# A new order table, four first transfers and 16 first fillers in a fused attention and gated-MLP kernel

## The chip, the core and the metric

The kernel runs on one core of one Trainium2 chip. The metric is the device time of one execution in microseconds; lower is better. The engines are named as in the profile: PE is TensorE (PEld its weight loads), DVE is VectorE, ACT is ScalarE, POOL is GpSimd, SP is SyncE, which only issues DMAs. DMAs that ScalarE issues show as ACTq, those of SP as SPq.

## What is computed

Attention with four sink positions and a window of 128, on 4 batches of 8 heads, 768 positions and 64 dimensions, then a gated MLP on its output (cut from the reference):

```python
scores = scale * np.matmul(q, k.transpose(0, 1, 3, 2))
keep = (pos[None, :] < n_sink) | ((rel >= 0) & (rel < window))      # n_sink 4, window 128
a = softmax(np.where(keep, scores, -1e9))
x = np.matmul(a, v)                       # -> (4, 768, 512)
h = np.maximum(x @ w_in, 0.0)             # 512 -> 1024
u, v = h[..., :512], h[..., 512:]
v_n = (v - mean(v)) / np.sqrt(var(v) + 1e-06)
v_s = np.einsum('ts,bsd->btd', w_spatial, v_n) + b_spatial[None, :, None]
out = (u * v_s) @ w_out                   # 512 -> 512
```

## The kernel before

**Stages.** A batch has six blocks of 128 positions; a step is one block and four of the eight heads, 48 steps in all. For each step TensorE makes the score products (L776) from `kring`, a ring of four blocks of keys and queries; VectorE adds the mask and takes the minimum (`mask`, L781); ScalarE takes the exponential (`exp`, L786); the result is split into a high and a low half of 16 bits (`p high`, `p low`, the low one at L511), turned by DMA transposes that SP issues (L852), and multiplied with `v` (`av`, L900). VectorE divides (L908), and the block `x` is split and turned in the same way. Steps 0 to 3 are turned on TensorE (`p cross`, `x cross`) instead. Then follow, for each block, `ps_v` = x @ w_in (its second half), `v relu`, `v stats` (L1005), `v root` on POOL (L1012), `v norm` (L1015: subtract the mean, multiply with the root), and the halves `vn high` and `vn low`; and, by chunks of 256 positions and 128 columns, `ps_u` (L529), `u relu` (L1049), `ps_s` with the spatial weights (L529), `gate` (L1072, adds the bias, on VectorE), `times` (L1076), `g high` (L679 on VectorE and POOL, L677 on ScalarE), `g low` (L1084), the output product `ps_o` (L1099), its copy `o copy` into a buffer `ob` (L1112, on ScalarE) and its store. The weights come in as `dec`, and are split into halves as well. Beside that stand tests of the inputs (`w check`, `v check`) whose result, the check, picks a general path at the end when the fast one would not be exact (it is not taken here).

**Rooms.** `ps_v`, `ps_u`, `ps_s`, `ps_o` and the turns on TensorE share two PSUM banks. `vr`, `ob` and two kinds of scratch (`junk`, `wtmp`) share a ring of three buffers in SBUF. A tile takes the room of an earlier one, and its first writer waits for the last reader of that one.

**What sets the order.** All work between the first loads and the end is recorded as 1799 pieces, numbered as they are recorded, each with the engines that can do it. The string `ORDER` lists them: a word is the number of a piece and the letter of its engine (P is TensorE, d VectorE, a ScalarE, p POOL, S SP). `Plan.order` walks it, and each engine's queue holds its pieces in this order; an engine whose next piece waits does nothing else. The costs given to `plan.add` aren't used when the kernel is built. A number behind P asks for as many fillers ahead of the piece: `warm` (L440) issues dummy matmuls of 128 x 248 into the bank of the piece itself, or of the piece named behind the colon. The first keys and queries are loaded ahead of everything else (L1190), by one DMA on SP's queue (head pairs 0 and 1) and one on ScalarE's (pairs 2 and 3).

Of the kernel before, what the change touches and what calls it, by code (L numbers as in the profile page):

```python
# [13 lines left out]
ALU = mybir.AluOpType  # L14
# [4 lines left out]
DM, DFF = 512, 1024  # L19
P = 128  # L20
# [179 lines left out]
NS = 4  # L200
# [4 lines left out]
NEG = -1.0e30  # L205
# [16 lines left out]
def cost(e, n, two=False, pointer=False):  # L222

    if e == "a":
        return 0.1 + n / 1200 + (0.1 if pointer else 0)
    if e == "d":
        return 0.085 + n / (960 if two else 1920) + (0.05 if pointer else 0)
    return 0.17 + n * 0.0018 if two else 0.14 + n * 0.001
# [5 lines left out]
116S 120P20 121d 123d 125d 117S 118p 257p 156p 119p 107S 108a 109a 21S 126a 127d 128a 111S 112a 110d 132P6:131  # L234
137d 139d 122a 124a 129P3 135d 22a 23d 133d 113a 136a 24d 25p 209p 114d 155S 159P1:131 164d 162d 140a 166d 130a
138a 134a 42S 141P2 160d 43a 44d 165a 115S 45d 46p 14S 131P 16d 163a 173P 180d 178d 174d 167a 161a 168P 142a 26a
176d 170P 143P 17d 15a 18p 208S 212P 144d 213d 215d 181a 217d 219d 179a 28S 30d 169a 47a 48d 313p 171a 154S 157p
0S 2d 177a 175a 216a 29a 31d 32p 214a 3d 184P15 218a 220a 185a 223a 1a 4p 182P 228P 233d 221a 183d 224d 235d 231d
229d 7S 9d 8a 35S 37d 236a 36a 207S 210a 230a 10d 11p 234a 256S 232a 239a 240p 225d 172P 145P 186P 187d 237a 49S
260P5 261d 38d 146a 50a 51d 39p 311S 314a 267d 33a 12a 188P9 189a 58S 263d 222S 265d 266a 241d 158d 211d 190a  # L240
268a 226S 255S 147P 148a 262a 264a 271a 269a 191d 52d 53p 272p 34d 276P 279d 258a 280a 227P 283d 284a 281d 282a
277d 192P 259d 273d 315d 312S 316P 319d 323d 321d 242S 317d 238S 243P 244d 245P23 278a 285a 289p 332P 287a 288p
5a 360S 6d 54a 40a 41d 27d 55d 270S 274S 275P 324a 322a 318a 339d 320a 193a 325a 286S 290S 246a 503S 327a 19a
333d 337d 340a 338a 334a 199P 326S 335d 247d 361p 364P 329p 328d 330S 336a 343a 344p 341a 13d 20d 504p 505p 345p
367d 368a 365d 200a 371d 369d 291P 56S 359S 292d 149d 342S 150p 151p 201P 346S 202a 380P 381d 550p 366a 370a 372a
373a 377p 57S 387d 383d 385d 382a 384a 194d 195p 293P 386a 294a 295d 375a 196p 248P 376d 508P 515d 513d 331P 509d
# [999 lines left out]
```

## Time and profile before

| | |
|---|---|
| three runs | 401.38, 401.75, 401.91 us (median 401.75) |
| the profiled execution | 401.43 us, span 399.6 us |
| busy in the span | PE 97%, DVE 78%, ACT 63%, POOL 53% |
| TensorE's mean granted clock | 0.999 of 2.4 GHz |
| fillers | 84, of which 20 ahead of the first score |

The span runs from the first to the last instruction. Each engine works through its own queue in order, so its idle time is read together with what ended it: in a timeline row the brackets give the idle time before the instruction and the engine, tile and line that released it. In the view of waits the releaser is the one that came last by the profile. Busy time of TensorE includes the fillers.

### The profile page before, as it was taken

The page shows a single profiled execution, that of the slowest core. Times are in us where ns is not written, and L with a number is a line of the kernel's source. Part 1 is how long each engine was busy: PE and PEld are TensorE (multiplying, and loading weights), DVE is VectorE, ACT ScalarE, POOL GpSimd, SP SyncE. Part 2 cuts the span into 40 slices and gives each one's busy share as a digit, 9 for nine tenths or more (in the row PEclk, how much of TensorE's full clock was granted, in tenths as well). Part 3 has the DMA queues.
Part 4 walks back from the last instruction along what each step waited for, and adds up shares of the span by engine and source line. Part 5 has one row for each costly group of instructions (what it writes and reads, how often), then busy time and mean ns, then how long its engine had stood idle before and what let it go on. Part 6 is the DMA issues. An engine that isn't in the chain of part 4 may idle for free. (4 is left out here: it accounts for less than half of the span.)

```text
span 399.6 us, 9923 instructions
## 1 busy us (share of the span) xinstructions
PE 387.3 (97%) x3697; PEld 276.4 (69%) x3697; DVE 312.4 (78%) x924; ACT 250.8 (63%) x553; POOL 210.5 (53%) x237
## 2 busy tenths in 40 slices
PE   7999998998999999999999999999999998999995
PEld 4785866686786774677777666777768666486773
DVE  3899999879888787989798897989896998342421
ACT  3999897877879476688796979888621131101010
POOL 4463596874552526454515478499666392720000
PEclk9999999999999999999999999999999999999999
DMA  6999999999895998869888979899799653001021
GB/s 194 384 284 218 196 183 230 256 251 219 205 228 135 242 188 192 214 153 144 165 173 210 207 186 267 143 189 147 168 237 232 185 175 85 27 2 53 2 80 57
DMA packets 137733, 70.96 MB, mean 178 GB/s; under 512 B 112080, under 2 KB 125392, under 8 KB 137680
## 3 DMA queue, kind: packets, MB, share of 16 engines
q1 hardware_dynamic: 136864, 70.02, 77.9%
q8 instruction: 30, 0.49, 0.5%
q10 hardware_dynamic: 816, 0.26, 0.3%
q14 instruction: 23, 0.19, 0.2%
HBM read 36.71 MB, written 6.29 MB: 108 GB/s over the span
## 5 line engine op out<-in xcount | busy, mean ns | idle before, releaser
L529 PE MATMUL ps_s<-wsp,vn 128*128 128x256 f16 x864 | 100.3, 273 | 0.7 <-ACT ob L1112 0.7
L786 ACT ACTIVATE pexp<-pexp,nm 128x260 f32<-128x260 f32 (+1 forms) x192 | 85.3, 484 | 18.6 <-DVE nm L781 18.2
L529 PEld LDWEIGHTS <-vn 128*128 128x128 f16 x864 | 83.1, 98 | 14.1 <-issue 2.2
L511 POOL TENSOR_TENSOR p<-pexp,p 128x1024 f16<-128x1024 f32 (+2 forms) x43 | 54.8, 1280 | 44.7 <-ACT p L495 35.7
L529 PE MATMUL ps_u<-xT,win 128*128 128x256 f16 x576 | 68.8, 273 | 1.6 <-DVE g L1072 1.1
L1099 PE MATMUL ps_o<-wout,g 128*128 128x512 f16 x276 | 62.9, 379 | 0.7 <-ACT ob L1112 0.7
L529 PEld LDWEIGHTS <-win 128*128 128x128 f16 x576 | 55.0, 98 | 11.4 <-issue 3.9
L529 PE MATMUL ps_v<-win,xT 128*128 128x512 f16 x264 | 60.5, 380 | 0.1
L1099 PEld LDWEIGHTS <-g 128*128 128x128 f16 x276 | 26.3, 98 | 30.1 <-issue 1.6
L776 PE MATMUL sc<-kring 64*128 64x260 f16 (+3 forms) x480 | 44.7, 312 | 1.3 <-DMA kring<-qk_t 1.2
L529 PEld LDWEIGHTS <-xT 128*128 128x128 f16 x264 | 24.8, 98 | 28.5 <-issue 1.5
L495 ACT CAST p<-pexp 128x32 f16<-128x32 f32 (+2 forms) x69 | 42.7, 639 | 2.7 <-DMA pT<-p 2.0
L1072 DVE SCALAR_TENSOR_TENSOR g<-ps_s,b_bc 128x256 f32<-128x256 f32 x48 | 20.2, 420 | 28.7 <-PE ps_s L529 28.6
L1015 POOL TENSOR_SCALAR vr<-vr,mv,rs 128x512 f32<-128x512 f32 x18 | 38.4, 2136 | 0.8
L1076 POOL TENSOR_TENSOR g<-g,u 128x256 f32<-128x256 f32 x22 | 17.4, 792 | 33.8 <-DVE g L1072 33.1
L1049 ACT ACTIVATE u<-ps_u 128x256 f32<-128x256 f32 x34 | 12.8, 378 | 34.2 <-PE ps_u L529 34.1
L900 PE MATMUL av<-vring,pT 128*128 128x65 f16 x328 | 34.2, 194 | 0.0
L901 PE MATMUL av<-vring,pT 128*128 128x65 f16 x328 | 34.1, 193 | 0.0
L902 PE MATMUL av<-vring,pT 128*128 128x65 f16 x328 | 34.1, 193 | 0.0
L511 DVE TENSOR_TENSOR p<-pexp,p 128x1024 f16<-128x1024 f32 (+2 forms) x33 | 27.0, 820 | 6.3 <-ACT p L495 6.2
L900 PEld LDWEIGHTS <-pT 128*128 128x128 f16 x328 | 30.3, 97 | 1.8 <-issue 0.8
L1084 DVE SCALAR_TENSOR_TENSOR g<-g,g 128x256 f16<-128x256 f16 x48 | 23.0, 484 | 10.0 <-POOL g L679 7.1
(144 smaller groups left out, 693.4 us busy)
## 6 DMA issues: line engine op xcount, KB each, us to landing
vraw<-v_s SPq DMA_DIRECT2D x30, 260.0 KB, 4.1
raw<-qk_t SPq DMA_DIRECT2D x12, 512.0 KB, 4.1
out<-ob SPq DMA_DIRECT2D x23, 256.0 KB, 2.3
kring<-qk_t SPq DMA_DIRECT2D x11, 512.0 KB, 5.6
dec<-w_in SPq DMA_DIRECT2D x8, 512.0 KB, 8.1
pexp<-w_in SPq DMA_DIRECT2D x8, 512.0 KB, 4.4
wsp<-w_sp_t SPq DMA_DIRECT2D x6, 384.0 KB, 4.1
dec<-w_out SPq DMA_DIRECT2D x4, 512.0 KB, 4.6
```

What stands on the lines that cost most here:

```text
L495: nc.scalar.copy(o, x)
L511: eng[e].tensor_tensor(out=o, in0=x, in1=hi, op=ALU.subtract)
L529: nc.tensor.matmul(o, a, m, start=(i == 0), stop=(i == n - 1))
L776: nc.tensor.matmul(view(h + q)[0], qq[:, hp, 1, 2:], keys, start=(j == 0), stop=(j == len(pairs) - 1))
L786: nc.scalar.activation(po, po, AF.Exp, bias=nm()[:, q:q + 1], scale=-1.0)
L900: nc.tensor.matmul(o[:, h], ph, vh, start=(t < 2 and j == 0), stop=False)
L901: nc.tensor.matmul(o[:, h], ph, vl, start=False, stop=False)
L902: nc.tensor.matmul(o[:, h], pl, vh, start=False, stop=(j == nb - 1 and (t < 2 or h == HH - 1)))
L1015: eng[e].tensor_scalar(vr(), vr(), vals["mv", i][:, 0:1], vals["rs", i], op0=ALU.subtract, op1=ALU.mult)
L1072: nc.vector.scalar_tensor_tensor(out=g(), in0=tl("ps_s", i)[:, :TC], scalar=G_S, in1=b_bc[:, t0:t0 + TC], op0=ALU.mult, op1=ALU.add)
L1084: plan.add("g low", r, b, "d", cost("d", TC, True), lambda e: nc.vector.scalar_tensor_tensor(out=g2()[:, 1], in0=g2()[:, 0], scalar=-2.0 * ...
L1099: nc.tensor.matmul(o, lead, wout[:, w, d, :], start=(d == 0 and j == 0), stop=(d == KC - 1 and j == 2))
```

## The change

`ORDER` is a new table: other places, and for some pieces another engine. In all DVE has 615 pieces (596 before), ACT 489 (508), POOL 213, PE and SP as many as before. By kind: `v norm` DVE 11 and POOL 13 (6 and 18 before); `p low` DVE 25 and POOL 19 (20 and 24); `vn high` ACT 6, DVE 6, POOL 12 (13, 3, 8); `vn low` DVE 6, POOL 18 (10, 14); `g high` ACT 16, DVE 16 (23, 9), POOL 16 as before; `u relu` ACT 32, DVE 16 (34, 14); `times` DVE 28, POOL 20 (26, 22). There are 65 fillers at eleven places (84 at nine): 16, 8, 1, 1, 6, 2, 5, 8, 1, 13 and 4, after 20, 6, 3, 1, 2, 15, 5, 9 and 23. On TensorE the order changes by neighbours changing places; from the output products of batch 2's second chunk on, about 328 us in the trace of before, it is the same. The costs in the code are set to other numbers. The first keys and queries come by four DMAs of 128 KB, one for each pair of heads, on SP's and ScalarE's queues in turn. The mask of the first block is made by one instruction on 124 columns. The line numbers after are one lower from L374 on. Of the table and of the costs one line each stands here:

```diff
-116S 120P20 121d 123d 125d 117S 118p 257p 156p 119p 107S 108a 109a 21S 126a 127d 128a 111S 112a 110d 132P6:131
+116S 120P16 127d 128a 117S 118p 125d 123d 21S 22a 23d 107S 121d 124a 132P8:143 139d 137d 111S 126a 108a 122a
...
-    def cur_mask(m):
-        nc.gpsimd.affine_select(out=m, in_=m, pattern=[[-1, P]], compare_op=ALU.is_ge,
-                                fill=NEG, base=0, channel_multiplier=1)
+    def cur_mask(m, first=0):
+        nc.gpsimd.affine_select(out=m, in_=m, pattern=[[-1, P - first]], compare_op=ALU.is_ge,
+                                fill=NEG, base=-first, channel_multiplier=1)
...
-    cur_mask(m_first)
-    nc.gpsimd.memset(m_first[:, :NS], 0.0)
+    cur_mask(m_first[:, NS:], NS)
...
-            plan.add("v norm", r, b, "dp", {"d": 0.46, "p": 0.75}, norm, [("st", i)], [("vr", i)], shared=True)
+            plan.add("v norm", r, b, "dp", {"d": 0.47, "p": 2.05}, norm, [("st", i)], [("vr", i)], shared=True)
...
-            for e, hs in ((nc.sync, slice(0, HP // 2)), (nc.scalar, slice(HP // 2, HP))):
-                e.dma_start(kring[:, 0, hs, :, 2:], qk[0, 0, :, hs])
+            for h in range(HP):
+                (nc.sync, nc.scalar)[h % 2].dma_start(kring[:, 0, h:h + 1, :, 2:], qk[0, 0, :, h:h + 1])
```

SP's queue at the start, before (`dec` are loads of w_in, `vsraw` and `vraw` of v; rows of engine instructions in their order, line first):

```order
L1190 DMA kring_63<-qk_t 128x4x128
L523 DMA vsraw_180<-v_sink 96x260
L523 DMA dec_184<-w_in 128x1024
L523 DMA vsraw_189<-v_sink 96x260
L740 DMA kring_63<-qk_t 128x8x128
L523 DMA dec_254<-w_in 128x1024
L523 DMA vraw_269<-v_s 128x520
```

and after:

```order
L1189 DMA kring_63<-qk_t 128x2x128 x2
L522 DMA dec_175<-w_in 128x1024
L522 DMA vsraw_181<-v_sink 96x260
L522 DMA vsraw_206<-v_sink 96x260
L739 DMA kring_63<-qk_t 128x8x128
L522 DMA dec_251<-w_in 128x1024
L522 DMA dec_280<-w_in 128x1024
L522 DMA vraw_282<-v_s 128x520
```

The load of a whole block of keys and queries (128x8x128) stands behind two `vsraw` in both, but now they are the fourth and fifth DMA of the queue, and two `dec` stand between it and the first `vraw`.

POOL's queue around the normalisation of the last block of batch 0 (`vr_1327` before, `vr_1317` after; `p16` is written by `p low`), before:

```order
L511 TENSOR_TENSOR p16_1_131<-pexp_1190,p16_1_131 128x1024
L748 COPY kring_63<-ksink_129 128x4x2
L1012 TENSOR_TENSOR rs_1346<-rs_1346,mhalf_111 128x1
L511 TENSOR_TENSOR vn_1383<-vr_1214,vn_1383 128x512
L1015 TENSOR_SCALAR vr_1327<-vr_1327,mv_1344,rs_1346 128x512
L511 TENSOR_TENSOR vn_1478<-vr_1327,vn_1478 128x512
L556 TENSOR_TENSOR w32_1490<-w32_1490,wtmp_1542 128x512
L511 TENSOR_TENSOR p16_1_131<-pexp_1387,p16_1_131 128x16
```

and after:

```order
L503 TENSOR_SCALAR vn_1341<-vr_1203 128x512
L510 TENSOR_TENSOR vn_1341<-vr_1203,vn_1341 128x512
L747 COPY kring_63<-ksink_130 128x4x2
L1011 TENSOR_TENSOR rs_1338<-rs_1338,mhalf_112 128x1
L503 TENSOR_SCALAR vn_1385<-vr_1317 128x512
L510 TENSOR_TENSOR vn_1385<-vr_1317,vn_1385 128x512
L747 COPY kring_63<-ksink_130 128x4x2
L555 TENSOR_TENSOR w32_1470<-w32_1470,wtmp_1496 128x512
```

The normalisation of that block (L1015 before) has left POOL, which now has both halves of its `vn` (L503, L510); `v norm` of `vr_1317` is on VectorE.

ScalarE's queue at the last output copies of batch 2 (`junk` is a row of the check, `u` is written by `u relu`), before:

```order
L606 ACTIVATE junk_5643,checks_139<-vraw_5274 128x512
L677 ACTIVATE g2_5652<-g_5440 128x256
L1112 ACTIVATE ob_5672<-ps_o_5659 128x512
L1112 ACTIVATE ob_5708<-ps_o_5695 128x512
L677 ACTIVATE g2_5755<-g_5752 128x256
L999 ACTIVATE vr_5819<-ps_v_5820 128x512
L1112 ACTIVATE ob_5873<-ps_o_5860 128x512
L1112 ACTIVATE ob_5894<-ps_o_5881 128x512
```

and after:

```order
L605 ACTIVATE junk_5623,checks_140<-vraw_5621 128x512
L1111 ACTIVATE ob_5647<-ps_o_5634 128x512
L494 CAST x16_5659<-x_5628 128x512
L1111 ACTIVATE ob_5681<-ps_o_5668 128x512
L600 ACTIVATE junk_5705,checks_140<-wsp_128 128x768
L998 ACTIVATE vr_5745<-ps_v_5746 128x512
L998 ACTIVATE vr_5797<-ps_v_5798 128x512
L1048 ACTIVATE u_5597<-ps_u_5812 128x256
L1111 ACTIVATE ob_5849<-ps_o_5836 128x512
L1111 ACTIVATE ob_5872<-ps_o_5859 128x512
```

A `u relu` (`ps_u_5812`) now stands between the copies of the first and the second chunk, and its bank is the one that the product read by `ob_5872` takes; before, that `u relu` was on VectorE, and the products read by `ob_5873` and `ob_5894` lay in the same bank.

## Rows read from the trace of the kernel before

**Rows 1.** the page's first part: busy us (share of the span) and instructions

```profile
PE 387.3 (97%) x3697; PEld 276.4 (69%) x3697; DVE 312.4 (78%) x924; ACT 250.8 (63%) x553; POOL 210.5 (53%) x237
```

**Rows 2.** what TensorE waited for: us in total, times, longest us

```profile
PE sc L776 <- DMA kring<-qk_t: 1.2, 2, 1.0
PE ps_u L529 <- DVE g L1072: 1.1, 1, 1.1
PE ps_o L1099 <- ACT ob L1112: 0.7, 1, 0.7
PE ps_s L529 <- ACT ob L1112: 0.7, 1, 0.7
PE ps_u L529 <- ACT u L1049: 0.4, 1, 0.4
```

**Rows 3.** three stretches: us, busy time by engine, PEclk, DMA share, GB/s

```profile
10.00:40.00 30.00, 29.81 (x238) 21.43 (x239) 28.22 (x91) 29.90 (x65) 14.58 (x14) 1.00 1.08 295
60.00:100.00 40.00, 37.59 (x368) 27.47 (x367) 34.80 (x109) 31.39 (x67) 26.65 (x25) 1.00 1.07 238
100.00:300.00 200.00, 199.56 (x2091) 140.00 (x2090) 173.71 (x504) 152.16 (x344) 115.62 (x119) 1.00 0.90 190
```

**Rows 4.** timeline, TensorE and SP, 0:42 us: start, us, instruction

```profile
1.73 4.31 PE L440 MATMUL sc<-ident 128*128 128x248 f16 x20 [1.73 <-POOL ident masks.py:199]
5.98 0.82 PE L776 MATMUL sc<-kring 64*128 64x128 f32 x8
10.67 1.15 PE L776 MATMUL sc<-kring 64*128 64x260 f32 x8
39.51 2.60 PE L440 MATMUL pt<-ident 128*128 128x248 f16 x23
...
0.72 0.45 SPq L1190 DMA_DIRECT2D kring<-qk_t  x1
2.70 0.67 SPq L740 DMA_DIRECT2D kring<-qk_t  x1
```

**Rows 5.** DMAs issued in 0:12 us: count, KB, median us to landing

```profile
kring<-qk_t SPq DMA_DIRECT2D x1, 256.0 KB, 3.9
kring<-qk_t ACTq DMA_DIRECT2D x1, 256.0 KB, 4.2
```

**Rows 6.** timeline, SP and TensorE, 59 to 65 us

```profile
59.39 0.60 SPq L740 DMA_DIRECT2D kring<-qk_t  x1
...
64.31 1.15 PE L776 MATMUL sc<-kring 64*128 64x260 f32 x8 [0.99 <-DMA kring<-qk_t]
```

**Rows 7.** timeline, GpSimd, ScalarE and TensorE, 83 to 93 us

```profile
83.26 2.89 POOL L1015 TENSOR_SCALAR vr<-vr,mv,rs 128x512 f32<-128x512 f32 x1
...
86.18 0.62 ACT L495 CAST vn<-vr 128x512 f16<-128x512 f32 x1 [2.36 <-POOL vr L1015]
...
92.21 1.03 PE L529 MATMUL ps_u<-xT,win 128*128 128x256 f16 x8 [1.13 <-DVE g L1072]
```

**Rows 8.** groups by line: busy us, mean ns of one, idle before

```profile
L1015 POOL TENSOR_SCALAR vr<-vr,mv,rs 128x512 f32<-128x512 f32 x18 | 38.4, 2136 | 0.8
L1015 DVE TENSOR_SCALAR vr<-vr,mv,rs 128x512 f32<-128x512 f32 x6 | 3.3, 542 | 1.0 <-POOL rs L1012 1.0
L511 POOL TENSOR_TENSOR p<-pexp,p 128x1024 f16<-128x1024 f32 x20 | 42.2, 2109 | 24.1 <-ACT p L495 24.0
L511 DVE TENSOR_TENSOR p<-pexp,p 128x1024 f16<-128x1024 f32 x18 | 22.0, 1223 | 2.9 <-ACT p L495 2.9
L511 DVE TENSOR_TENSOR vn<-vr,vn 128x512 f16<-128x512 f32 x10 | 6.8, 688 | 0.0
L679 DVE TENSOR_SCALAR g<-g 128x256 f16<-128x256 f32 x9 | 2.6, 293 | 3.9 <-POOL g L1076 3.8
```

**Rows 9.** timeline, ScalarE, 326 to 347 us

```profile
326.57 0.63 ACT L606 ACTIVATE junk<-vraw 128x512 bf16<-128x512 f32 x1 [2.30 <-DVE vr L634]
...
345.75 0.60 ACT L1112 ACTIVATE ob<-ps_o 128x512 f32<-128x512 f32 x1 [3.30 <-DVE u L1051]
```

More of the change, by code (lines that the diff above doesn't have):

```diff
@@ L227, in cost @@
         return 0.085 + n / (960 if two else 1920) + (0.05 if pointer else 0)
[L228 removed]
+    return 0.2 + n * 0.00182 if two else 0.14 + n * 0.00087
 ORDER = """
[L234 to L236 removed]
@@ L237 @@
[L237 to L246, printed above, removed]
@@ L555, in decode @@
                 [("dec", i)], [("w32", i)], shared=True)
-            plan.add(name, step, 0, "p", 1.27, lambda e: nc.gpsimd.tensor_tensor(
+            plan.add(name, step, 0, "p", 1.23, lambda e: nc.gpsimd.tensor_tensor(
                 out=ci(), in0=ci(), in1=tl("wtmp", i), op=ALU.add), [("wtmp", i)], [("w32", i)])
@@ L747, in queries_keys @@
             c = 2 * (t % 2)
-            plan.add("k copy", r, b, "p", 0.17, lambda e: nc.gpsimd.tensor_copy(
+            plan.add("k copy", r, b, "p", 0.155, lambda e: nc.gpsimd.tensor_copy(
                 *((room16[:, :, :, 0, :2], sinks[:, :, :, c:c + 2]) if halves else (room[:, :, 0, :2], ksink[:, :, c:c + 2]))),
@@ L790, in scores @@
                 keys = [(f"kslot{kslot(0, 0)}", (0, 0), (0, hf))]
-            plan.add("score", i, b, "PE", (0.78 if t else 0.45) if b >= B16 else 1.08 if t else 0.75, product, keys, banks)
+            plan.add("score", i, b, "PE", (0.86 if t else 0.53) if b >= B16 else 1.17 if t else 0.74, product, keys, banks)
             for q in range(n):
@@ L820, in weights_f32 @@
                 plan.add("p cross", i + 0.01 * k, b, "PE", 0.5, cross, [("pexp", i)], [bank, ("pT", i, (2, k))])
-                plan.add("pt copy", i + 0.01 * k, b, "ad", {"a": 0.52, "d": 0.62}, copied, [bank],
+                plan.add("pt copy", i + 0.01 * k, b, "ad", {"a": 0.468, "d": 0.605}, copied, [bank],
                          [("pT", i, (2, k))])
@@ L948, in split_turned @@
             plan.add("x cross", i, b, "PE", 0.55, cross, [("x", (b, t))], [bank, (*key, t % 2)])
-            plan.add("x high", i, b, "ad", {"a": 0.53, "d": 0.62}, upper, [bank], [(*key, t % 2)])
-            plan.add("x low", i, b, "d", 0.62, lambda e: nc.vector.tensor_tensor(
+            plan.add("x high", i, b, "ad", {"a": 0.508, "d": 0.605}, upper, [bank], [(*key, t % 2)])
+            plan.add("x low", i, b, "d", 0.605, lambda e: nc.vector.tensor_tensor(
                 out=half(1), in0=raw(), in1=half(0), op=ALU.subtract), [bank], [(*key, t % 2)])
@@ L965, in turned @@
             plan.add("x cross", i, b, "PE", 0.55, cross, [("x", (b, t))], [bank, (*key, t % 2)])
-            plan.add("x copy", i, b, "ad", {"a": 0.52, "d": 0.62}, copied, [bank], [(*key, t % 2)])
+            plan.add("x copy", i, b, "ad", {"a": 0.468, "d": 0.605}, copied, [bank], [(*key, t % 2)])
             if t % 2 == 0:
```

178 lines of the change are left out of this document (95 added, 83 removed).

## The prediction

> **What bounds the kernel now.** The page's first part comes first: TensorE is busy 387.3 of 399.6 us [rows 1], so whatever the change does to the other engines, time can be won only where TensorE waits, or in work that it does for nothing. The view of what it waited for says how much that is: five lines of 0.4 to 1.2 us and no long one, for DMAs of queries and keys (`kring`), VectorE's `gate`, two output copies and a `u` copy [rows 2]. Added up they are 1.2 + 1.1 + 0.7 + 0.7 + 0.4 = 4.1 us. The table of stretches says which engine stands next: in 10 to 40 us ScalarE is busy 29.90 of 30 us, VectorE 28.22, and the DMA share is over 1; in 100 to 300 TensorE loses 0.44 of 200 us while VectorE is busy 173.71, so it has some 26 us of idle time there and GpSimd some 84 [rows 3]. The "useless" work is fillers, dummy matmuls of `warm`: 84 before. The first twenty take 4.31 us, 23 later ones 2.60 [rows 4]; less the 0.16 us by which the last one of a row runs on after its start spacing, that is 0.207 and 0.106 us each, TensorE's lower level (1.2 GHz) and its upper (2.4). The execution shown took 401.43 us: span 399.6 and 1.83 around it. It lies 0.32 us below the median of 401.75; I make the sum as differences and take them from the median.
>
> **The change, part by part.**
>
> *Fillers and first transfers.* 84 fillers become 65: four cold ones go (4 x 0.207 = 0.83 us) and, of 64 warm ones, 15 (15 x 0.106 = 1.59 us), together 2.4 us of TensorE time. That is the upper end. It is a gain only where the work behind the filler was ready earlier. It was at the start: of the two first transfers of 256 KB SP's was issued at 0.72 [rows 4] and took 3.9 us, ScalarE's 4.2 [rows 5], so the keys lay there at 4.6 to 5, and the first score began at 5.98, straight after the fillers [rows 4]. With 16 fillers it can begin at 1.73 + 16 x 0.207 = 5.04. It was not at the next place: the second score came at 10.67, and it waits for the next load, issued at 2.70 [rows 4]. In the new order SP issues that load behind both `vsraw` loads, the second of which waits for the completion of a first transfer; by the landing above that is after 4.6 us rather than at 2.70. The later places in the ramp (the 23 before `x cross`, now 13) stand where ScalarE is full [rows 3] and TensorE was waiting for it; a filler taken away there becomes a wait. So the bounds are -2.4 (all) and +1.0 (the load 2 us later, half of it passed on), and I take -0.6, a little below the cold part, since that is the only part of which a row shows that the work was ready. Four transfers of 128 KB in place of two cost one more issue on SP and one on ScalarE's queue, 0.45 us each by the row at 0.72 [rows 4]; only loads that are needed much later stand behind them, but for the one just priced, so nothing is added.
>
> The Trainium skill's "DMA: Bandwidth & Descriptors", section "Issuing engines are not separate DMA queues", speaks against this part: starting transfers from several engines saves only sequencer time, as they run on the same 16 DMA engines. The trace agrees as far as it goes, the two old ones, from two engines, having taken 3.9 and 4.2 us side by side [rows 5]. By that rule the first keys would land no earlier and the start would be worth 0 instead of -0.6.
>
> *Load 14.* A score at 64.31 had waited 0.99 us for `kring`. Its load was issued at 59.39 [rows 6], behind the two transposes of step 10 in SP's queue, and these waited for that step's `p low` on GpSimd, 2.11 us as a rule [rows 8]. In the new order the load stands behind the same two transposes, but this `p low` is on VectorE, 1.22 us [rows 8]: 0.9 us earlier if VectorE comes to it in time. I take -0.8; bounds 0 and -1.0. The other `kring` wait, 1.2 - 1.0 = 0.2 us [rows 2], goes with it: -0.2.
>
> *The gate of 90 us.* The row to read is a normalisation of a `v` block on GpSimd at 83.26 that took 2.89 us. ScalarE stood idle 2.36 us for it with four exponentials queued behind, these let a `p low` come late, and `gate` stands behind that in VectorE's queue, for which TensorE waited 1.13 us until 92.21 [rows 7]. The same operation takes 0.54 us on VectorE [rows 8], where the new order puts it, with the high half of `vn` on GpSimd instead of ScalarE, so that no exponential stands behind either. -1.1. What is late next is the same gate behind the p low of that step; between them and TensorE's need stand two score products and an `av`, so I leave it at zero and put the price into the term on VectorE.
>
> *The `u` copy of 175 us.* TensorE waited 0.4 us for a `u` copy on ScalarE [rows 2]. ScalarE has 19 pieces fewer in the new order (489 after 508), so I take this as gone: -0.4, bounds 0 and -0.4.
>
> *The tail.* Two waits of 0.7 us on `ob` [rows 2]. In the second, two output products stand in a row in one PSUM bank, since the `u` copy between them, on VectorE, came free later than the output copy: the product has to wait for that copy, 345.75 to 346.35 [rows 9]. The new order has this `u` copy on ScalarE and the second product in the other bank: -0.7, bounds 0 and -0.7. In the first, the output copy has to wait until its buffer has been stored from the copy before it. Buffer and store are the same in the new order; but the copy before it was late, since ScalarE had stood 2.30 us for VectorE in the check's row ahead of it [rows 9]. The new order also has a row of the check there, which may or may not be late: bounds 0 and -0.7, taken -0.4.
>
> *VectorE's added work.* Against these gains stand 19 more pieces on VectorE. By the rows [rows 8]: five `p low` 5 x 1.22 = 6.1; five normalisations 5 x 0.54 = 2.7; seven `g high` 7 x 0.29 = 2.0; four `vn low` fewer, 4 x 0.69 = 2.8 off; and net six others, at least 0.29 each, 1.7. Together 9.7 us. GpSimd loses ten long pieces (5 x 2.14 + 5 x 2.11 = 21 us) and takes `vn` work back. The 26 us of VectorE's idle time in 100 to 300 us cover 9.7, if they lie where it is needed. The nearest row for what it costs when they do not is 60 to 100 us, where VectorE is busy 34.80 of 40 [rows 3] and one gate was late by 1.1 [rows 2]. With 9.7 more, 100 to 300 goes from 87% to 92%, so I price one such stall and one like that of 175 us: +1.5. Lower end 0 (the idle time hides all), upper end +4.9 (half of it shows).
>
> Sum: -0.6 - 0.8 - 0.2 - 1.1 - 0.4 - 0.7 - 0.4 + 1.5 = -2.7; 401.75 - 2.7 = **399.0 us** (399.05). With every gain whole and nothing for VectorE, -2.4 - 1.0 - 0.2 - 1.1 - 0.4 - 0.7 - 0.7 = -6.5: 395.2.
>
> **The rivals.**
>
> *VectorE becomes the bound (slower).* For it: it is the next busiest engine over the whole of 10 to 300 us, already 28.22 of 30 in the ramp [rows 3], and the change gives it more. Masks stand on it, and every exponential waits for a mask. Against it: its idle time is mostly waiting for TensorE. If half of the 9.7 us shows (+4.9) and the ramp's gains go (the -0.6 and -0.8 above), it is 401.75 - 2.8 + 4.9 = 403.9. It decides as soon as more than 4.2 us of the added work, the sum of the gains, is not covered.
>
> *The ramp takes nothing and stalls move (no change).* The fillers turn into waits, the later load costs 1.0 at the second score, load 14 is still behind its transposes, and VectorE costs its 1.5: 401.75 - 0.2 - 1.1 - 0.4 - 0.7 - 0.4 + 1.0 + 1.5 = 401.5. For it: the full DMA and ScalarE of 10 to 40 us [rows 3]. Against it: at the start the keys lay ready for 0.9 us.
>
> *The clock (no change).* The rate of the fillers doubled between the first twenty and the rest [rows 4]; the score at 5.98 still ran close to that turn. With four cold ones fewer, the eight products of the first score may run at the lower level (+0.8), and 15 fewer later leave 1.6 us of waits in which the level may fall, work behind them taking twice as long: +1.6 if it falls for as long as that. 399.0 + 2.4 = 401.4. Against it: 49 warm fillers remain in the same stretches. The Trainium skill's "TensorE: Matmul & The Clock Gate", section "What's actually happening", calls the throttled state the default one, from which activity releases the engine, which is this rival's mechanism; the rows on the fillers agree with a slow start, and no row before shows a fall.
>
> **How the numbers follow.** Forecast 0.66; stalls move 0.14; clock 0.06; VectorE bound 0.14. A difference of 0.2% (0.8 us) is about what a measurement of this kernel tells from none: faster is below 400.95, slower above 402.55. All of the forecast and a fifth of the two middle ones are faster: 0.70; the rest of these is the same: 0.16; VectorE's rival is slower: 0.14. The range runs from 395.2, all gains whole, to 403.2, inside the last rival; what lies outside is about 0.15.
>
> **What would show it.** Right, step by step: 16 fillers and a first score at about 5.0; the second score no later than 10.7; no `kring` wait over 0.3 us near 62; no wait on a gate near 90, with the normalisation there on VectorE at about 0.55 us; no `ob` wait near 345; VectorE busy some 322 us, with the waits on it in 100 to 330 us adding to 1.5 or less. Wrong: a second score after 11.5, a row of waits on `mask`, `gate` or `u` in 100 to 330 us that adds to over 4, or a granted clock below 1 in 10 to 40 us.

## The result, and the profile after

The changed kernel is slower: 403.52 us (median) against 401.27 of the kernel before on the same chips, a ratio of 1.0062, 95% interval 1.0046 to 1.0079. The forecast was 399.0, faster; the range ended at 403.2. The profiled execution of after took 403.24 us, span 401.4, so 1.8 us longer than the one shown of before. Three of after's executions, in which the granted clock was 0.998 or more on the mean, took 401.4 to 401.6 us; in the others it was lower, and they took 402.5 us or more.

The first part of the page and what TensorE waited for (us in total, times, longest), to be held against [rows 1, 2]:

```profile
PE 388.3 (97%) x3678; PEld 276.6 (69%) x3678; DVE 323.2 (81%) x943; ACT 244.7 (61%) x534; POOL 206.9 (52%) x236
```

```profile
PE sc L775 <- DVE nm L780: 2.5, 1, 2.5
...
PE sc L775 <- ACT kring L496: 1.3, 1, 1.3
PE sc L775 <- DMA kring<-qk_t: 1.1, 2, 0.6
PE sc L439 <- DVE nm L780: 0.6, 1, 0.6
PE ps_row L659 <- DVE good L656: 0.5, 1, 0.5
PE pt L959 <- DVE x L909: 0.4, 1, 0.4
PE ps_o L1098 <- DVE u L1050: 0.3, 1, 0.3
PE ps_s L528 <- DVE g L1071: 0.2, 1, 0.2
```

All the waits of [rows 2] but those on `kring` are gone. In their place stands a wait of 2.5 us on a mask (`nm` is its minimum) and one of 1.3 on ScalarE's split of `kring`. VectorE is busy 10.8 us more, where the prediction counted 9.7.

[Rows 2] leave out a wait of 1.0 us in the head of before, for exponentials that stood behind ScalarE's split of the second `vsraw` (view of waits, and timeline of ScalarE, 5 to 14 us, before):

```profile
PE pt L815 <- ACT pexp L786: 1.0, 1, 1.0
```

```profile
8.88 0.42 ACT L696 ACTIVATE vsink<-vsraw 96x256 f16<-96x256 f32 x1 [0.70 <-DMA vsraw<-v_sink]
```

Where the time goes is seen by comparing, in the two traces, when TensorE ends the same set of pieces ("lag": after minus before; each from one profiled execution):

| place | lag, us | step |
|---|---|---|
| first score, 6.8 us | -0.52 | -0.52 |
| `av` of step 1, 16.7 us | +4.15 | +4.67 |
| `x cross` of step 5, 42.5 us | +3.25 | -0.90 |
| score of step 14, 65.5 us | +3.12 | -0.13 |
| `ps_u`, 93.7 us | +2.11 | -1.01 |
| score of step 23, 130.2 us | +3.50 | +1.39 |
| `ps_u`, 178.1 us | +2.96 | -0.54 |
| `ps_o`, 329.0 us | +3.92 | +0.96, in several steps |
| `ps_o`, 349.2 us | +2.34 | -1.58 |

The loss is made within the first 17 us. From 43 us on the new order wins 0.9 us net, as the last line less the third says. The head of after, timeline of all engines, 0 to 13 us (start, us, instruction):

```profile
0.72 0.97 SPq L1189 DMA_DIRECT2D kring<-qk_t  x2
...
1.73 0.47 SPq L522 DMA_DIRECT2D dec<-w_in  x1
1.73 3.49 PE L439 MATMUL sc<-ident 128*128 128x248 f16 x16 [1.73 <-POOL ident masks.py:199]
...
2.24 1.84 SPq L522 DMA_DIRECT2D vsraw<-v_sink  x2
...
4.12 0.67 SPq L739 DMA_DIRECT2D kring<-qk_t  x1
...
5.15 1.12 PE L775 MATMUL sc<-kring 64*128 64x128 f32 x8
...
9.59 0.68 ACT L547 ACTIVATE wtmp<-dec 128x512 int32<-128x512 uint32 x1 [2.41 <-DMA dec<-w_in]
9.59 0.43 DVE L549 TENSOR_SCALAR w<-dec 128x512 int32<-128x512 int32 x1 [2.43 <-DMA dec<-w_in]
...
9.94 0.28 DVE L780 CUSTOM_DVE_ANT_0 pexp<-sc,m_first 128x128 f32<-128x128 f32 x1
...
10.38 0.76 PE L775 MATMUL sc<-kring 64*128 64x128 f32 x2 [2.51 <-DVE nm L780]
```

The first score starts at 5.15 where it started at 5.98 [rows 4], as forecast; it takes 1.12 us instead of 0.82, so it ends only 0.52 earlier. Then VectorE and ScalarE come to the split of the first `dec`, whose load was issued at 1.73 and has landed only just before 9.59. The masks stand behind it in VectorE's queue, and the last two products of the second score (step 1's) wait for room that these masks free. The second `vsraw` is issued at 3.8 to 4.1 (two issues, 1.84 us together) and the key block at 4.12, not at 2.70 [rows 4].

The prediction counts the scores otherwise: what it calls the second, at 10.67 in before, is that of step 2, the first of the second block; step 1's, at 7.47 in before, is not in [rows 4]. Step 2's came at 12.76 in after.

### The profile page after: what moved, and what is told of

The parts are those of the page before. It is cut to its first block, busy times and chain, and to the rows that moved or that the text cites. A ratio compares the mean times of both kernels' runs of the same rounds, so it can differ in the third digit from the quotient of the medians.

```text
span 401.4 us, 9882 instructions
## 1 busy us (share of the span) xinstructions
PE 388.3 (97%) x3678; PEld 276.6 (69%) x3678; DVE 323.2 (81%) x943; ACT 244.7 (61%) x534; POOL 206.9 (52%) x236
## 5 line engine op out<-in xcount | busy, mean ns | idle before, releaser
L510 POOL TENSOR_TENSOR p<-pexp,p 128x16 f16<-128x16 f32 (+2 forms) x40 | 46.3, 1162 | 26.2 <-ACT p L494 22.1
L1075 POOL TENSOR_TENSOR g<-g,u 128x256 f32<-128x256 f32 x20 | 16.2, 809 | 69.1 <-DVE g L1071 58.3
L775 PE MATMUL sc<-kring 64*128 64x260 f16 (+3 forms) x480 | 46.7, 319 | 5.0 <-DVE nm L780 2.5
L494 ACT CAST p<-pexp 128x1024 f16<-128x1024 f32 (+2 forms) x67 | 40.4, 621 | 2.3 <-DMA pT<-p 1.2
L555 POOL TENSOR_TENSOR w<-w,wtmp 128x512 int32<-128x512 int32 x12 | 16.5, 1372 | 36.8 <-DVE w L552 20.1
L1111 ACT ACTIVATE ob<-ps_o 128x512 f32<-128x512 f32 x23 | 13.7, 594 | 34.3 <-PE ps_o L1098 31.7
L510 DVE TENSOR_TENSOR p<-pexp,p 128x1024 f16<-128x1024 f32 (+2 forms) x36 | 33.7, 943 | 0.6 <-ACT p L494 0.4
L899 PEld LDWEIGHTS <-pT 128*128 128x128 f16 x328 | 30.3, 97 | 1.8 <-issue 0.6
L900 PEld LDWEIGHTS <-pT 128*128 128x128 f16 x328 | 30.1, 97 | 0.8
```

What stands on the lines that cost most here:

```text
L494: nc.scalar.copy(o, x)
L510: eng[e].tensor_tensor(out=o, in0=x, in1=hi, op=ALU.subtract)
L555: plan.add(name, step, 0, "p", 1.23, lambda e: nc.gpsimd.tensor_tensor(out=ci(), in0=ci(), in1=tl("wtmp", i), op=ALU.add), [("wtmp", i)], ...
L775: nc.tensor.matmul(view(h + q)[0], qq[:, hp, 1, 2:], keys, start=(j == 0), stop=(j == len(pairs) - 1))
L899: nc.tensor.matmul(o[:, h], ph, vh, start=(t < 2 and j == 0), stop=False)
L900: nc.tensor.matmul(o[:, h], ph, vl, start=False, stop=False)
```

## Experiments

Each ratio is to the kernel before on the same chip, with its 95% interval, from five rounds; "lag" is as above, against the same trace of before. Executions of one kernel differ: those of before took 398.25 to 403.81 us, and the second trace of it (below) has a lag of +1.88 against the first. A lag of that size in one trace is therefore not yet an effect of an edit; the ratios, from many executions, decide.

### Which part of the change costs: the start alone, its two halves, and after without it

The start of after in the kernel before (both edits), and each edit by itself:

```diff
-116S 120P20 121d 123d 125d
+116S 120P16 121d 123d 125d
...
-            for e, hs in ((nc.sync, slice(0, HP // 2)), (nc.scalar, slice(HP // 2, HP))):
-                e.dma_start(kring[:, 0, hs, :, 2:], qk[0, 0, :, hs])
+            for h in range(HP):
+                (nc.sync, nc.scalar)[h % 2].dma_start(kring[:, 0, h:h + 1, :, 2:], qk[0, 0, :, h:h + 1])
```

> The kernel before with only the start of the changed one: four transfers of 128 KB on two queues, and 16 first fillers instead of 20; the order is that of before. Head theory: the first score begins at 5.1 instead of 6.0, the second score still waits for its load; 400.6 to 401.4, that is -0.6 to 0. Rival, the start costs the time (the clock rises later or the loads come later): 402 to 404.

> The kernel before with the four first transfers and its own 20 first fillers. Counter theory: as slow as with 16 fillers, 1.005 to 1.007 of before. Rival, the fillers: 1.000.

> The kernel before with 16 first fillers and its own two transfers. Counter theory: 0.998 to 1.001 of before. Rival, the fillers: 1.005 to 1.007, with a granted clock below 1 in 10 to 20 us.

Both edits: 1.0061 (1.0038 to 1.0084). Four transfers with 20 fillers: 1.0030 (1.0002 to 1.0057). Sixteen fillers with two transfers: 1.0007 (0.9987 to 1.0027). The start alone is as slow as the whole change, and the fillers alone cost nothing. With 20 fillers the four transfers cost half as much, where as much as with 16 was expected; the intervals overlap, so whether the fillers add to it is not settled. With four transfers TensorE again has a long wait in the head, this time behind exponentials that stand behind ScalarE's split of `vsraw` (timeline of the kernel with both edits, 5 to 14 us, ScalarE):

```profile
7.10 0.42 ACT L696 ACTIVATE vsink<-vsraw 96x256 f16<-96x256 f32 x1 [2.81 <-DMA vsraw<-v_sink]
```

The reverse, after with the two old transfers (the diff's last four lines turned round):

> The changed kernel with the two first transfers of 256 KB of before in place of the four of 128 KB; order and 16 fillers as changed. Counter theory (ten DMAs are issued before the first has landed in place of eight, there are eight completion counters, so the second vsraw and the load behind it wait for the first transfer, 4.1 us instead of 2.7, and everything that needs them comes late): 2 to 3.5 us less than the changed kernel, 0.996 to 1.001 of before. Rival, the 16 fillers (TensorE waits, the clock falls): no gain, 1.006. Rival, VectorE's added work: no gain, 1.006.

1.0016 (0.9992 to 1.0040), lag +0.63 at `av` of step 1 instead of +4.15. So after is slow only with the four transfers; what they meet in the head comes below. With them taken back the new order is still no faster than before.

### Not the order of the first splits, not the clock

In the new order the first split of `dec` (pieces 22 and 23) stands ahead of two first masks. Moved behind them in after, and the reverse in before:

```diff
-116S 120P16 127d 128a 117S 118p 125d 123d 21S 22a 23d 107S 121d 124a
+116S 120P16 127d 128a 117S 118p 125d 123d 21S 107S 121d 124a
...
-129P1 112a 140a 133d 113a 156p 119p 135d 136a
+129P1 112a 140a 133d 113a 156p 119p 22a 23d 135d 136a
```

> The changed kernel with one edit: the first split of a w_in chunk (pieces 22 on ScalarE and 23 on VectorE) goes behind the first eight masks again, instead of standing ahead of the fourth. Head theory (the split waits for its load with masks queued behind it, TensorE waits 2.5 us and then works at its lower clock): the lag of 3.6 us that the trace of after shows at 45 us against before goes almost whole; about 400.0 us, 3.0 to 4.0 below the changed kernel, and a granted clock of 1.00 in 10 to 20 us. Rival, VectorE's added work costs the time all through: no change, about 403.5. Rival, the four transfers and the 16 fillers cost it: at most 1 us is won, 402.5 or more.

> The kernel before with the same pieces moved the other way: 22 and 23 ahead of the fourth mask. Its load is issued at 1.77 us and lands at about 8.5. Head theory: the fourth mask and the second score behind it come 1.5 to 2.5 us later, and the clock falls in that wait or not; 402.8 to 404.8. Rivals: the order of the first masks doesn't matter, since ScalarE and the DMAs set the ramp; 401.3 as before.

After with late splits: 1.0081 (1.0057 to 1.0105), no gain; before with early ones: 1.0008 (0.9988 to 1.0028), no loss. In the first, TensorE's wait goes from 2.5 us on a mask to 2.8 on an exponential, which stands behind the next late load (the view of waits, and ScalarE's timeline, 5 to 14 us):

```profile
PE pt L814 <- ACT pexp L785: 2.8, 1, 2.8
```

```profile
10.02 0.42 ACT L695 ACTIVATE vsink<-vsraw 96x256 f16<-96x256 f32 x1 [2.33 <-DMA vsraw<-v_sink]
```

So it is not one load at a bad place: the first `dec` and both `vsraw` come late.

After its wait, TensorE runs at the lower of its two levels. The stretches of after (us, busy time by engine, granted clock, DMA share, GB/s):

```profile
8.00:9.00 1.00, 0.00 (x0) 0.00 (x0) 0.00 (x0) 0.00 (x0) 0.00 (x0) 1.00 0.90 226
...
10.00:11.00 1.00, 0.62 (x2) 0.50 (x2) 0.23 (x3) 1.00 (x4) 0.00 (x0) 0.50 1.08 366
...
16.00:17.00 1.00, 1.00 (x8) 0.69 (x8) 0.71 (x2) 1.00 (x3) 0.11 (x1) 0.86 1.07 359
```

Two kernels put fillers in: 32 instead of 8 ahead of the second score, and 22 within it, ahead of the products that wait.

```diff
-107S 121d 124a 132P8:143 139d 137d
+107S 121d 124a 132P32:143 139d 137d
```

```diff
+                            if i == 1 and h + q == n - 1:
+                                key = plan.pieces[143][2][0]
+                                for _ in range(22):
+                                    nc.tensor.matmul(tl(*key[:2])[:, key[2], :248], st.ident.bitcast(F16)[:, :P],
+                                                     st.ident.bitcast(F16)[:, :248], start=True, stop=True)
                             nc.tensor.matmul(view(h + q)[0],
```

> The changed kernel with 32 fillers in place of 8 ahead of the second score: TensorE has work in the wait of 2.5 us at 8 to 10.4 us, and the wait itself stays. If the lower clock after the wait (0.50 from 9.5 to 16.3 us in the trace of after) costs time of its own, this gives 1 to 2 us back, 401.5 to 402.5. If only the wait costs, 403.5.

> The changed kernel with 22 more fillers inside the second score, ahead of its last product, just where TensorE waits 2.5 us for the fourth mask. The wait stays. If the lower clock after it costs time of its own: granted clock 1.00 in 10 to 20 us and 1.0 to 2.5 us faster than the changed kernel, 1.000 to 1.004 of before. If the wait alone costs: 1.006.

1.0080 (1.0056 to 1.0104) and 1.0061 (1.0037 to 1.0085). In the second the wait is filled and the clock kept (its stretch of 10 to 20 us, same columns):

```profile
10.00:20.00 10.00, 8.80 (x68) 6.61 (x67) 8.28 (x34) 8.83 (x25) 3.73 (x5) 1.00 1.07 382
```

and the time is that of after (1.0062). In the head the kept clock does win something: at 42.5 us these two traces lag by 0.97 and 1.28 us, where after's lags by 3.25. But at 93.7 us they lag by 1.75 and 2.31, where after's lags by 2.11: other waits have come in its place (0.8 us for a transpose of `p` at 49 us is one). So the lower clock costs nothing that is left in the time of the kernel. The Trainium skill's "TensorE: Matmul & The Clock Gate", section "What's actually happening", calls the throttled state the default; the rows at 0.50, which follow TensorE's wait, agree. That rival's price, 2.4 us, was not there in the time.

The kernel before, run once more for its trace:

> The kernel before, for a profile on the same chip as the other three. By every theory 1.000; the trace gives the start on this chip: vsraw landing, second score, clock.

403.46 us in that one execution, with a wait of 2.2 us behind an exponential in the head and a clock of 0.83 in 10 to 20 us. Its lag is +1.88 at `av` of step 1, and as much at the end. So the late loads come in an execution of the kernel before too. With four transfers, the scalars in their old place and no fillers in the gap, the longest wait there is 1.5 to 2.8 us in four traces; with two transfers it is 0.5 to 2.2 in eight. A long wait is therefore not the four transfers' alone; with them it is longer on the whole.

### What makes the first loads late: two loads of 1 KB

Ahead of the work `load_scalars` loads `n_sink` and `window` into all 128 partitions (`words`, two DMAs on ScalarE's queue, 128 packets of 8 bytes each), needed only by the check at the end. My theory at this point was the number of outstanding DMAs: the ninth DMA of the program, counted over both queues, is issued only when an early one has landed. The trace says why: the first eight signal eight different semaphores, the ninth signals that of the second DMA again and waits for it. So this is a wait of the program; that the chip has such a limit is not shown. In before the ninth is the second `dec` on SP's queue. The second DMA is the load of keys on ScalarE's queue, issued at 0.80, and lands 4.2 us later, at 5.0 [rows 5] (timeline of SP, before, and what SP waited for up to 14 us):

```profile
5.06 0.34 SPq L523 DMA_DIRECT2D dec<-w_in  x1
```

```profile
SPq L523 <- DMA kring<-qk_t: 1.7, 1, 1.7
```

In after, with two more ahead, the ninth is the second `vsraw`. To free two places the loads of the scalars were issued late, on SP's queue at some 16 us, in after, in before, in after with two transfers, and in before with the small loads of SP put ahead as well:

```diff
-            load_scalars(nc, words, n_sink, window)
...
+                if k == LATE:
+                    nc.sync.dma_start(st.words[:, 0:2], st.scalars[0].bitcast(I32).partition_broadcast(P))
+                    nc.sync.dma_start(st.words[:, 2:4], st.scalars[1].bitcast(I32).partition_broadcast(P))
```

> The changed kernel with its four first transfers, but the two loads of 1 KB (n_sink, window) are issued behind the first ten loads on SP's queue, so eight DMAs and no more stand ahead of the second block of keys. Counter theory: second vsraw issued before 3 us in place of 4, TensorE's wait at 8 us shorter, 1.5 to 2.5 us faster than the changed kernel, 1.000 to 1.002 of before, as with two transfers. Rival, the four small transfers are bad by themselves (their landing, their share of the DMA engines): 1.006.

> The kernel before with the two loads of 1 KB behind the first ten loads: two more loads (w_in, v) leave before the first has landed, at about 3.5 and 4 us instead of 5.06 and 5.45. If the counters bind in the kernel before too: 0.5 to 1.5 us less, 0.996 to 0.999. If its ramp is set by ScalarE and the DMA engines: 1.000.

> The changed kernel with two first transfers and the 1 KB loads late. Counter theory: the later loads leave as early as they can; no worse than with either alone, 0.996 to 1.000 of before. If it is 1.002 or more, what is left of the loss is the new order itself.

> As the run before this one, and on SP's queue both vsraw loads and the second block of keys stand ahead of the first 512 KB of w_in. If TensorE's wait near 8 to 9 us comes from the landing of the second vsraw (8.88 in the trace of before) and the second score's from its keys (10.53): both land 1.5 us or more earlier, 1 to 2 us less than before, 0.995 to 0.998. Rival: the w_in split comes later and the ramp ends no earlier, 1.000 or more.

After: 0.9999 (0.9972 to 1.0027), the loss is gone. Before: 0.9961 (0.9933 to 0.9988), faster than both kernels. After with two transfers: 0.9966 (0.9941 to 0.9990). Before with the small loads ahead: 0.9971 (0.9947 to 0.9996), no better. In before with the scalars late, the second `dec` and the first `vraw` go out at 3.43 and 4.12 (timeline of SP):

```profile
3.43 0.65 SPq L524 DMA_DIRECT2D dec<-w_in  x1
4.12 0.72 SPq L524 DMA_DIRECT2D vraw<-v_s  x1
```

This agreed with the theory, but the edit does two things at once: it takes away two outstanding DMAs, and 256 packets of 8 bytes. The trace of after speaks for the second: its first `dec`, issued ahead of any wait, landed just before 9.59, and just before 7.67 with the scalars late. So the last run kept two DMAs at the old place, of one packet each:

```diff
+            spare = top.tile([1, 4], I32, name="spare")
+            nc.scalar.dma_start(spare[:, 0:2], n_sink.bitcast(I32).partition_broadcast(1))
+            nc.scalar.dma_start(spare[:, 2:4], window.bitcast(I32).partition_broadcast(1))
```

> The changed kernel with the two loads of the scalars issued late as in e9_words_late, and in their old place on ScalarE's queue two loads of the same 8 bytes into one partition only (into a buffer that nothing reads): two DMAs as before, but 2 packets in place of 256. Theory A (the count of outstanding DMAs is the cause): SP's second vsraw is issued at about 4.1 us as in the changed kernel, everything behind it lands late, TensorE waits some 2.5 us at 8 to 10 us, ratio 1.004 to 1.008. Theory B (the 256 packets of 8 bytes are the cause: while they are under way, 2.5 to 10 us in the changed kernel, the DMA engines move 100 to 230 GB/s, and the first dec, issued at 1.73 ahead of any wait on a queue, lands at 9.59 where it landed at 7.67 without them): the second vsraw is issued at 4.1 as well, but the first dec has landed by 7.7 us, the longest wait of TensorE in the head is about 1 us, ratio 0.998 to 1.002.

0.9980 (0.9954 to 1.0007). The second `vsraw` is issued as late as in after, yet the first `dec` is there at 8.19 and TensorE's wait is 1.6 us (timeline of SP and ScalarE, view of waits):

```profile
2.24 1.89 SPq L523 DMA_DIRECT2D vsraw<-v_sink  x2
```

```profile
8.19 0.68 ACT L548 ACTIVATE wtmp<-dec 128x512 int32<-128x512 uint32 x1 [1.53 <-DMA dec<-w_in]
```

```profile
PE sc L776 <- DVE nm L781: 1.6, 1, 1.6
```

So my theory of the count fell as the main cause: with the count unchanged, the loss is gone. The view of DMA traffic in 4.5 to 9.5 us (packets, MB, rate; below it the share of the DMA engines' time, q1 being SP's queue and q10 ScalarE's) shows what the packets do, in after

```profile
DMA packets 1058, 0.85 MB, mean 171 GB/s; under 512 B 294, under 2 KB 951, under 8 KB 1058
...
q1 hardware_dynamic: 805, 0.85, 58.9%
q10 hardware_dynamic: 253, 0.00, 2.5%
```

and with single packets

```profile
DMA packets 1432, 1.35 MB, mean 270 GB/s; under 512 B 67, under 2 KB 1279, under 8 KB 1432
...
q1 hardware_dynamic: 1428, 1.35, 96.8%
```

The packets of 8 bytes take 2.5% of the DMA engines' time by the records, but while they are under way SP's loads fall from 96.8% to 58.9%. That the packets and not the count of DMAs hold the other loads up is shown by this pair of runs; how they do it is not. The same row of the other kernels:

| kernel | transfers | scalars | GB/s, 4.5 to 9.5 us | ratio |
|---|---|---|---|---|
| after | four | early | 171 | 1.0062 |
| after's start in before | four | early | 205 | 1.0061 |
| after, two transfers | two | early | 196 | 1.0016 |
| before | two | early | 228 | 1 |
| after, single packets | four | late | 270 | 0.9980 |
| after, scalars late | four | late | 282 | 0.9999 |
| before, scalars late | two | late | 293 | 0.9961 |
| after, two, scalars late | two | late | 314 | 0.9966 |

All four with the early scalars move less than all four without; so it is in all 20 traces, 170 to 228 against 270 to 320. Among the early ones the rate does not order the times (196 and 205 stand beside 1.0016 and 1.0061). The landing of the second block of keys orders the groups better: 12.55 us in after, 10.96 in after's start, 10.5 in the two with two transfers, 9.2 to 10.2 in the four with the scalars late. The Trainium skill's "DMA: Bandwidth & Descriptors", section "Specifications", gives 512 bytes as the least transfer for full rate; the trace agrees for packets of 8: by the rows of after one of them takes 8 ns of a DMA engine (2.5% of 16 x 5 us for 253), 1 byte per ns, where SP's, of 1056 bytes on the mean, move 18. The traces add that the loads beside them pay.

How four transfers bring it out: with two, the first `dec` of after's order is issued at 1.23 and the second `vsraw` by 2.67, and `dec` has landed at 6.1 (4.9 us later); with four, `dec` goes out at 1.73 and `vsraw` waits until 3.8, so that more of both falls into the stretch with the small packets. That is read from the traces; of the late issue alone, the run with single packets against that with the scalars late says it costs 0.5 us (lag at `av` of step 1 +0.70 and +0.18), and the ratios don't tell the two apart. Issued late on SP's queue, at 16.4 and 18.3 us in after, the same packets move at 22.3 to 24.3 us; the rate in 22 to 24 us is 319 GB/s, where it is 355 in after with the scalars early and 347 in before. So they cost about a tenth there, where early they cost more than a third, and for 2 us instead of 5. Whether the second queue or the place in time makes the difference was not tried.

Not all of the gain in before is in the head. The lag with the scalars late is -0.59 at `av` of step 1 and -0.56 at 42.5 us; it reaches -2.74 at 93.7 by steps at 65, 74 and 92 us, of which the last, -1.2, is the gate of the next part.

### The gate of 90 us

The prediction put this wait down to the normalisation on GpSimd. In before, that one piece was moved to VectorE; then also the `vn high` behind it to GpSimd:

```diff
-565S 404p 651S
+565S 404d 651S
```

```diff
-566P 655P 405a 624a
+566P 655P 405p 624a
```

> The kernel before with one letter changed: the normalisation of the last block of batch 0 on VectorE instead of GpSimd. If that normalisation is the cause of the gate's wait at 90 us: the wait of 1.1 us goes in the trace, and 0.5 to 1.1 us in the time, 0.997 to 0.999. If not, the gate still waits and the time is 1.000.

> The kernel before with the normalisation of the last block of batch 0 on VectorE (as in the run before) and, too, the high half of its vn on GpSimd instead of ScalarE. Second theory of the gate at 90 us (not the long normalisation, but that ScalarE's next piece waits for it with exponentials behind): the wait of 1.1 us goes in the trace, 0.997 to 0.999 of before. Rival (VectorE's own queue ahead of the gate): the wait stays, 1.000 to 1.003.

1.0028 (1.0003 to 1.0052) and 0.9988 (0.9967 to 1.0009). With the first alone the normalisation takes 0.54 us, and the wait on the gate stays (timeline of VectorE and ScalarE, 82 to 93 us, and the view of waits):

```profile
84.58 0.54 DVE L1015 TENSOR_SCALAR vr<-vr,mv,rs 128x512 f32<-128x512 f32 x1
...
85.15 0.62 ACT L495 CAST vn<-vr 128x512 f16<-128x512 f32 x1 [2.53 <-DVE vr L1015]
```

```profile
PE ps_u L529 <- DVE g L1072: 1.1, 1, 1.1
```

On VectorE the piece comes later in the queue, so ScalarE's `vn high` starts at 85.15 instead of 86.18 and has waited as long (2.53, 2.36 in [rows 7]), with the exponentials behind. With `vn high` off ScalarE as well the wait is gone; lag -1.3 at that place.

That does not yet show `vn high` to be the cause, and the intervals of the two ratios overlap. In three kernels that change only the start, with these pieces as in before, the wait is gone too (both edits; four transfers) or is 0.4 us (16 fillers), and the lag falls by 1.3, 1.3 and 0.7 at the same place. There the normalisation on GpSimd took 2.08 us instead of the 2.89 of [rows 7], and ScalarE stood 1.0 to 1.5 us for it (both edits, timeline of GpSimd and of ScalarE, 80 to 96 us):

```profile
84.68 2.08 POOL L1015 TENSOR_SCALAR vr<-vr,mv,rs 128x512 f32<-128x512 f32 x1
...
86.79 0.62 ACT L495 CAST vn<-vr 128x512 f16<-128x512 f32 x1 [1.26 <-POOL vr L1015]
```

In nine traces with `vn high` on ScalarE, TensorE waits 0.9 to 1.2 us for the gate where ScalarE stood 2.3 to 2.5 us ahead of `vn high` (four traces), and 0.4 or nothing where it stood 1.0 to 1.5 (five). So the gate follows the time that ScalarE stands there, and a normalisation that ends earlier removes the wait as moving `vn high` does. Why the same instruction took 2.9 us in some executions and 2.1 in others was not tried.

Both together with the late scalars, in before:

> The kernel before with the two parts that helped it singly, put together: the two 1 KB loads of the scalars issued late (0.9961 by itself), and the normalisation of the last block of batch 0 on VectorE with its vn high on GpSimd (0.9988 by itself, 1.1 us less in the trace at 90 us). Theory A (the gains add, since they lie at different places: the head, and 90 us): 0.9961 - 0.0012 to 0.0028, so 0.993 to 0.995, and a span below 396.3 us. Theory B (the loads that come earlier have already taken the wait at 90 us away, since the lag of that kernel grew from -1.2 at 67 us to -2.7 at 97 us): no wait on a gate near 90 us in either, and the same 0.996 as without the second edit.

0.9947 (0.9927 to 0.9968), the fastest kernel of this study, though its interval overlaps that of the late scalars alone (0.9961). In that one's trace the wait on the gate had gone too (normalisation 2.08 us), so whether the gains add is not settled.

### The middle of the order alone

Before's order up to 46 us and from 300 us, after's between, with two transfers; at the end the `u` copy of step 45 is on ScalarE as in after:

> An order put together: that of before up to about 46 us (two first transfers, 20 first fillers), then that of the changed kernel up to about 300 us, then that of before again, with the u copy of step 45 on ScalarE. Prediction's mechanisms (load 14, the gate of 90 us, the u copy of 175 us, the bank in the tail) hold: 1.4 to 2.2 us less than before, 0.9945 to 0.9965. Rival, VectorE's added work takes them back: 1.000 or more.

1.0028 (1.0002 to 1.0053), where a gain was expected. The trace has +1.9 us of lag at the seam, 50 to 55 us, where a `ps_v` waits 1.5 us for a `u relu`, and -1.3 at 92 us and -0.9 at 346. The seam was mine, so the ratio does not price the middle. The gain at 92 us is also seen with before's pieces there (above); the one at 346 comes with the `u` copy on ScalarE.

## Why the prediction was wrong

*Fillers and first transfers: -0.6 forecast (bounds -2.4 and +1.0), +3.25 by the lag at 42.5 us.* This is the step that failed. Its first half held: 16 fillers, a first score that starts 0.8 us earlier. The failed sentence is that behind the two more issues "only loads that are needed much later stand". The first `dec` and the `vsraw` stand behind them, and these are needed at 7 to 10 us by splits that have masks and exponentials in line behind. In before they cost 1.0 us already, the wait that [rows 2] leave out, so the head looked freer than it was. The later key block, which I priced, was not what ended last, but only just: it landed at 12.55 where it had landed at 10.53, right ahead of step 2's score at 12.76. And the upper bound took the load's delay by its issue, where the rate of the DMA engines fell as well; nothing in the prediction looked at the two 1 KB loads, though [rows 3] showed the DMA share over 1 right after and the head's own share could have been asked for. What stood in its place: with the two 1 KB loads late, or with single packets in their place, the same four transfers lag by 0.18 and 0.70 us at `av` of step 1, not 4.15, and cost nothing by the ratio. Two of the prediction's own signs of being wrong came true: step 2's score at 12.76, after 11.5, and a granted clock below 1 in 10 to 40 us.

By the Trainium skill's "DMA: Bandwidth & Descriptors", section "Issuing engines are not separate DMA queues", the start would be worth 0; that was nearer than my -0.6, and still on the wrong side. The traces agree with it on the first keys: with four transfers the last of them landed at 4.58 in after, with two at 4.55 to 4.83 in eleven traces and at 5.04 in the one of before that is shown.

*Load 14: -0.8 forecast, and -0.2 for the other `kring` wait.* The load was issued at 60.69 with the lag of the head in it, and its score waited 0.51 us instead of 0.99 (timeline of TensorE, 60 to 70 us, after); over that stretch the lag falls by 0.54.

```profile
66.85 1.15 PE L775 MATMUL sc<-kring 64*128 64x260 f32 x8 [0.51 <-DMA kring<-qk_t]
```

The earlier issue held; the load took 6.0 us to land instead of 4.8, so the gain was less. The other wait did not go, it grew from 0.25 to 0.62 us, at 77 us in after.

*The gate of 90 us: -1.1 forecast, -1.3 in the lag.* The forecast named both moves, and in after both are there (timeline of VectorE and GpSimd):

```profile
85.58 0.54 DVE L1014 TENSOR_SCALAR vr<-vr,mv,rs 128x512 f32<-128x512 f32 x1
...
86.21 0.62 POOL L503 TENSOR_SCALAR vn<-vr 128x512 f16<-128x512 f32 x1 [0.94 <-DVE vr L1014]
```

The size is in part luck: the 2.89 us of [rows 7] is that execution's, and where GpSimd took 2.08 the kernel before had nothing to win there.

*The `u` copy of 175 us: -0.4 forecast, -0.54 measured.* The size held.

*The tail: -0.7 and -0.4 forecast.* Both waits on `ob` are gone from the view. The lag moves by -0.86 at 331 and -0.89 at 346 us, more than forecast.

*VectorE's added work: +1.5 forecast.* The largest new wait, +1.39 at 130 us, is ScalarE's (timeline of ScalarE and of TensorE, 126 to 134 us):

```profile
129.19 0.63 ACT L605 ACTIVATE junk<-vraw 128x512 bf16<-128x512 f32 x1 [1.13 <-DMA out<-ob]
...
129.95 0.60 ACT L1111 ACTIVATE ob<-ps_o 128x512 f32<-128x512 f32 x1
130.44 0.62 ACT L496 ACTIVATE vring<-vraw 128x512 f16<-128x512 f32 x1
131.48 1.06 ACT L496 ACTIVATE kring<-raw 128x1024 f16<-128x1024 f32 x1 [0.41 <-DMA raw<-qk_t]
```

```profile
132.59 1.15 PE L775 MATMUL sc<-kring 64*128 64x260 f32 x8 [1.31 <-ACT kring L496]
```

A row of the check waits for the store that frees its buffer, and the split of the next keys stands behind it. That this is near 1.5 is chance. VectorE's own waits come later: 0.2 us for a gate and 0.3 for a `u relu`, lag +0.35 at 303 to 306 and +0.49 at 327 us. In the traces of the new order whose head is not late they are longer: 0.8 and 0.6 us with two transfers, 1.0 and 0.2 with the scalars late, 0.7 and 0.4 with single packets, none and 0.6 with two transfers and the scalars late. So the term was too small: in after ScalarE's and VectorE's steps come to 2.2 us by the lag. The rival "VectorE becomes the bound" gave 403.9, near the measured time, but not by its mechanism: with the same work on VectorE and two transfers after is at 1.0016, with the scalars late as well at 0.9966.

*The clock.* The price forecast for that rival was 2.4 us; the granted clock did fall, to 0.50 for 6.8 us. Filling the gap gave some 2 us back at 42.5 us and nothing in the time of the kernel.

In sum: 1.8 us slower in the two spans against 2.7 faster forecast; the head alone differs by 3.25 + 0.6 = 3.9 us, most of these 4.5. But the rest of the sum is not borne out either. With two transfers the changed kernel has all of the forecast's other terms, -2.1 us or 0.995, and came out at 1.0016 (0.9992 to 1.0040); with the scalars late too it is at 0.9966, where the kernel before is at 0.9961. By the ratios the new order itself wins nothing: what its traces gain at 65, 92, 175, 331 and 346 us they lose in part at 129, 303 and 327, and a part of the gain at 92 us before has by itself in other executions. How the rest divides is open.

## What to carry to other kernels

Before a first load is split, count what stands behind the added issues on the queue and is needed soonest, and look at the DMA rate of the head, not only at the landing of the load itself: tiny loads that nobody needs early belong behind the first work. A shorter operation removes a wait only if it also ends earlier: on VectorE the normalisation took 0.54 us instead of 2.89, but stood later in the queue, and the wait stayed. Before a wait is priced from one trace, look for it in a second trace of the same kernel: the one at 90 us is not in every execution. When two things leave with one edit, the run that puts one of them back is the one to make.

## What was not expected of the hardware

Two loads of 1 KB in packets of 8 bytes on ScalarE's queue held the loads beside them to 171 GB/s in 4.5 to 9.5 us, where these moved 270 with single packets in their place; they took 8.0 and 8.4 us to land, and their share of the DMA engines' time reads 2.5%. The same normalisation on GpSimd took 2.89 us in one execution of these pieces and 2.08 in another. And a granted clock of 0.50 for 6.8 us, which a filled gap avoided, made no difference to the time of the kernel (1.0062 and 1.0061).
